# Transformer block on one core: 80 of 2048 units of the softmax exponentials computed on VectorE instead of ScalarE

## The chip, the cores and the metric

The kernel runs on one core of a Trainium2 chip. The metric is the device time of one execution in microseconds; the median of the runs counts. Engines are named as in the profile: PE (TensorE, with PEld for its weight loads), ACT (ScalarE), DVE (VectorE), POOL (GpSimd), SP (SyncE, whose queue issues the DMAs here).

## The reference

One block without learned norm weights, in bf16, for a sequence of 2048 tokens and width 640: attention with 32 heads of 20 elements, then a gated product with inner width 1728. Both have a layer norm ahead of them and a residual around them.

```python
h  = x + A(layernorm(x))        # A: qkv = x @ wqkv; p = softmax(q k^T * 20**-0.5); (p v) @ wo
h2 = h + B(layernorm(h))        # B: ((x @ w_gate) * (x @ w_up)) @ w_down
```

There are 32 x 2048 x 2048 exponentials. There is no mask, and the kernel subtracts no maximum: it checks at the end that the sums are in range, and has a slow general version for the case that they aren't (not run with these inputs).

## The kernel before

**Heads.** Four heads form a head group, eight groups in all (`NG`). In `qa`, `qb` and `kT` each head has a slot of 32 partitions, 20 with data and 12 of padding, so that a group fills 128 partitions. The values `vx` have 20 columns of data and one of ones per head, so that the product with them also gives the softmax's sum.

**Units, tiles, segments, passes.** The scores are made transposed, keys on partitions. A unit is one head, 128 keys and 512 queries: one score matmul (line 392), 512 exponentials per partition, and one matmul with the values (line 483, "AV"). Three units fill a tile of 1536 columns: PSUM tile `sc`, double buffered, is read by one ScalarE instruction that writes `E` in bf16:

```python
nc.scalar.activation(e[:, 0:n], sc[:, 0:n], ACT.Exp, scale=SM_SCALE)     # line 398
```

A segment is one head group against all its keys for one block of 512 queries: 16 key tiles x 4 heads = 64 units, collected in PSUM tile `acc` (one buffer). Pass "0" covers queries 0 to 511, "1" and "2" the next blocks; the last block is done as "3" for groups 0 and 1 and in halves "A" and "B" for the others. In pass 0 the groups 0 to 3 are done by key chunks, while the keys are still being made, with partial sums in `parts`. That leaves 20 whole segments of 64 units in the passes 0, 1 and 2: 4 + 8 + 8. The whole has 2048 units in 683 tiles.

**The order around it.** The program is emitted by one loop over tiles, and each engine executes in the order of emission. An iteration emits the three score matmuls and the exponential of tile i (`emit_S`), then the rest of a started job up to 640 ns of matmul time (`go_on`, `BUDGET`), then four AV matmuls of an older tile (`emit_AV`), then a piece of auxiliary VectorE work (`step_aux`) and due events. If no job was under way, it begins the next one (`begin`, up to `START` = 440 ns). So a projection of five matmuls takes two iterations.

**Jobs.** All other matmul work is a queue of jobs: transposes of the normalised input, the q, k and v projections (`job_proj`, `job_V`), then for each finished block of queries the tail: output projection with residual into `h` (`job_out`, line 697), layer norm on VectorE in pieces (`ln2_pieces`, lines 162 to 207), transposes, the gated product (`job_glu`, lines 757 and 764) and the last product (`job_y`, line 792). Each sum of a job goes through the one PSUM bank `mi` and is evacuated by VectorE (`evac`, line 223), which frees the bank for the next job. If a tile of scores needs a q or k that isn't made, `ensure` emits its job at once.

**Normalisation.** A finished segment is copied from `acc` to `asb` (line 491); its sums go through DRAM, their reciprocals come back as `bc`, five and then eight tiles later (`norm`, `later`), and VectorE's product (line 422) writes the bf16 result `On`, of which there are two sets, for even and odd blocks of queries. In three places where there is no time for that, it is done with small matmuls (`job_norm`).

The residual of the tail is loaded into `xr` (bf16), `h` is a tile of its own in fp32, and the output is written over `xr`.

Of the kernel before, what the change touches and what calls it, by code (L numbers as in the profile page):

```python
# [51 lines left out]
LAG = 10  # L52
EARLY = 48


@with_exitstack
def kernel(
# [23 lines left out]
    ep = pool("ep", 6)  # L81
    nrm = pool("nrm", 2)
    small = pool("small", 2)
    accp = pool("accp", 1, space=bass.MemoryType.PSUM)
# [10 lines left out]
    ext = const.tile([P, 4], F32, name="ext")  # L95
    bad = const.tile([1, 1], I32, name="bad")
    wo = [const.tile([P, D], BF16, name=f"wo{g}") for g in range(NG)]
    N_SUMS = 16 * (NB * NG)
# [6 lines left out]
    vx = [vp.tile([P, VW], BF16, name=f"vx{t}") for t in range(NT)]  # L105
    On = [[onp.tile([P, QB], BF16, name=f"on{s}_{g}") for g in range(NG)] for s in range(2)]

    lnT = ra.tile([P, KT, S], BF16, name="lnT")
    wv = [ra.tile([P, D], BF16, name=f"wv{c}") for c in range(KT)]
    wqk = [ep.tile([P, EW], BF16, name="E") for c in range(KT)]  # L110
    parts = [ra.tile([P, QB], F32, name=f"part{g}") for g in range(G1)]
    wpad = [ra.tile([P, 2, H, SLOT], BF16, name=f"wp{c}") for c in range(KT)]
# [30 lines left out]
    warm = small.tile([P, 1], BF16, name="warm")  # L143
    nc.scalar.activation(warm[:], ones[:], ACT.Sqrt)
    for c in range(KT):
        nc.vector.memset(wpad[c][:].rearrange("p m h e -> p (m h) e")[:, :, DH:SLOT], 0.0)
# [61 lines left out]

    lns = {}

    def apply1(t, m32, r, k, eng=None):
# [7 lines left out]
    def evac(eng, dst, src):  # L219
        if eng == "act":  # L220
            nc.scalar.copy(dst, src)
        else:
            nc.vector.tensor_copy(dst, src)  # L223

# [60 lines left out]
    FAST = {("2", NG - 1), ("A", NG - 1), ("B", NG - 2)}  # L285

    tiles, cur_t, pos = [], [], 0
    for s, (p, g, lo, hi, _) in enumerate(segs):
        w = PASS[p][2]
        n = BANK // w  # L290
        for kt, j, k in [(kt, j, k) for kt in range(lo, hi, n) for j in range(HPG) for k in range(n)]:
            cur_t.append((s, kt + k, j, pos))
            pos += w
            if pos == EW:
                tiles.append((cur_t, EW))
                cur_t, pos = [], 0
    if cur_t:
        tiles.append((cur_t, pos))

    av_q = deque()  # L300
# [7 lines left out]
    cur = {"key": None, "gen": None, "fresh": True}  # L308
    now = {"i": 0}
    col = {"n": 0}  # L310
# [71 lines left out]
    def emit_S(i):  # L382
        sc = scp.tile([P, EW], F32, name="sc")
        us, n = tiles[i]
        for s, kt, j, _ in us:
            p, g = segs[s][0:2]
            ensure(("k", g, kt // TPB))
            ensure(("q", PASS[p][0], g))
        for s, kt, j, o in us:
            p, g = segs[s][0:2]  # L390
            b, c0, w = PASS[p]
            nc.tensor.matmul(  # L392
                sc[:, o:o + w],
                lhsT=kT[g][SLOT * j:SLOT * (j + 1), kt * P:(kt + 1) * P],
                rhs=q_of(g, b, c0, w)[SLOT * j:SLOT * (j + 1), :],
                start=True, stop=True)
        e = ep.tile([P, EW], BF16, name="E")
        nc.scalar.activation(e[:, 0:n], sc[:, 0:n], ACT.Exp, scale=SM_SCALE)  # L398
        for s, kt, j, o in us:
            av_q.append((i, s, kt, j, e[:, o:o + PASS[segs[s][0]][2]]))  # L400

    def norm(s, asb):
        p, g = segs[s][0:2]
        b, c0, w = PASS[p]
        n = w // 32
        r16 = sums_all[:, col["n"]:col["n"] + n]
        col["n"] += n
        sums = dram.tile([HPG, w], F32, name="sums", tag=f"sums{w}")
        nc.sync.dma_start(sums[:], asb[DH:P:SLOT, 0:w])
        nc.sync.dma_start(r16, sums[:].rearrange("j (c f) -> (j c) f", f=n))  # L410

        def back():
            ri = nrm.tile([P, n], F32, name="ri", tag=f"ri{n}")
            nc.vector.reciprocal(ri[:], r16)
            scr = dram.tile([HPG, w], F32, name="scr", tag=f"scr{w}")
            nc.sync.dma_start(scr[:].rearrange("j (c f) -> (j c) f", f=n), ri[:])
            bc = nrm.tile([P, QB], F32, name="bc")
            for j in range(HPG):
                nc.sync.dma_start(bc[SLOT * j:SLOT * (j + 1), 0:w], scr[j:j + 1, :].to_broadcast([SLOT, w]))

            def mult():
                nc.vector.tensor_tensor(On[b % 2][g][:, c0:c0 + w], asb[:, 0:w], bc[:, 0:w], ALU.mult)  # L422
                done.add(("n", p, g))
            later(8, mult)
        later(5, back)
# [21 lines left out]
    def job_norm(s, asb):  # L447
# [5 lines left out]
        ps = rows_to_cols(bc, w, bank())  # L453
        nc.vector.tensor_tensor(On[b % 2][g][:, c0:c0 + w], asb[:, 0:w], ps[:, 0:w], ALU.mult)
        done.add(("n", p, g))
# [4 lines left out]
    def emit_AV(upto):  # L460
        if not av_q:
            return
        i, s = av_q[0][0:2]
        p, g, lo, hi, kind = segs[s]
# [14 lines left out]
        for _ in range(ready):  # L479
            _, _, kt, j, e = av_q.popleft()  # L480
            ensure(("v", kt, g // (NG // 2)))
            h = HPG * g + j
# [4 lines left out]
        acc["left"] -= ready  # L487
        if acc["left"] == 0:
            if kind in ("copy", "only"):
                asb = parts[g] if kind == "copy" else nrm.tile([P, QB], F32, name="asb")  # L490
# [36 lines left out]
    keep_busy(WARM)  # L527

    def ln_bank(k):
# [41 lines left out]
    load_x(2)  # L571
    evac("act", kT[0][:, 0:QB], pK[:, 0:QB])
    evac("dve", q_of(0, 0, 0, QB), pQ[:, 0:QB])
    done.update({("q", 0, 0), ("k", 0, 0)})
# [114 lines left out]
    def out_mm(on, st, t):  # L689
        for hf in range(2):  # L690
            ps = bank()
            cs = slice(hf * HALF, (hf + 1) * HALF)
            for g in range(NG):
                nc.tensor.matmul(ps[:, 0:HALF], lhsT=on[g][:, t * P:(t + 1) * P], rhs=wo[g][:, cs],  # L694
                                 start=(g == 0), stop=(g == NG - 1))
                if g == NG - 1:
                    nc.vector.tensor_tensor(st["h"][t][:, cs], ps[:, 0:HALF], st["xr"][t][:, cs], ALU.add)  # L697
                yield 136
# [16 lines left out]
    def job_out(on, st, ts, key):  # L715
# [10 lines left out]
        for k, pair in enumerate(pairs):  # L726
            for t in pair:
                yield from out_mm(on, st, t)
            if k:
                yield from T_pair(pairs[k - 1])  # L730
# [21 lines left out]
    def glu_sum(st, fp, f2, k, c0, n, hold):  # L752
# [3 lines left out]
        for c in range(KT):  # L756
            nc.tensor.matmul(ps[0:M, 0:n], lhsT=st["w", fp][k][:, c, f2 * P:f2 * P + M],  # L757
                             rhs=st["ln2T"][:, c, c0:c0 + n], start=(c == 0), stop=(c == KT - 1))
            if c == KT - 1:
                if k == 0:  # L760
                    u = hold["u"] = late["s"].tile([P, QB], BF16, name="u")
                    evac("dve" if end["pool"] is None else "act", u[0:M, 0:n], ps[0:M, 0:n])
                else:
                    nc.vector.tensor_tensor(st["hh"][2 * fp + f2][0:M, c0:c0 + n], ps[0:M, 0:n], hold["u"][0:M, 0:n], ALU.mult)  # L764
            yield 216 * n // QB
# [15 lines left out]
    def job_y(st, ts, store_halves=False):  # L781
        for t in ts:
            o = st["xr"][t]
            for hf in range(2):
                ps = bank()
                cs = slice(hf * HALF, (hf + 1) * HALF)
                for f in range(2 * FP):
                    K = min(P, FF - f * P)
                    nc.tensor.matmul(ps[:, 0:HALF], lhsT=st["hh"][f][0:K, t * P:(t + 1) * P],  # L789
                                     rhs=late["Wd"][f][0:K, cs], start=(f == 0), stop=(f == 2 * FP - 1))  # L790
                    if f == 2 * FP - 1:
                        nc.vector.tensor_tensor(o[:, cs], ps[:, 0:HALF], st["h"][t][:, cs], ALU.add)  # L792
                    yield 136
# [14 lines left out]
    def add_tail(b, ts):  # L808
# [13 lines left out]
        do(("load",) + key, ready)  # L822
        add(("out",) + key, lazy(lambda st: job_out(On[b % 2], st, ts, key)))
        add(("glu",) + key, lazy(lambda st: job_glu(st, ts)))
# [26 lines left out]
    def last_tail():  # L851
        st = tail_st[LAST_B]
        on = On[LAST_B % 2]
        asb = final["asb"]
# [57 lines left out]
    def flag_ok():  # L912
# [7 lines left out]
        ok = small.tile([P, 1], BF16, name="ok", tag="den")  # L920
        nc.vector.tensor_tensor(ok[:], lo[:], hi[:], ALU.mult)
        return ok

# [12 lines left out]
    while i < n_tiles or av_q:  # L936
        now["i"] = i
        if i < n_tiles:
# [39 lines left out]
    def general():  # L978
        st = new_st(None)
        st["res"] = {}  # L980
        with tc.For_i(0, S, P) as r0:
# [3 lines left out]
            for g in range(NG):  # L985
# [41 lines left out]
                nc.tensor.transpose(ps[:], oq[:].rearrange("p j e -> p (j e)"), ident[:])  # L1027
                nc.vector.tensor_copy(On[0][g][:, 0:P], ps[:])
            for fn in (job_out(On[0], st, [0], None), job_glu(st, [0]), job_y(st, [0])):
                for _ in fn:  # L1030
# [34 lines left out]
```

## Time and profile before

| | us |
|---|---|
| median of 3 runs (lowest, highest) | 998.93 (998.02, 999.89) |
| the profiled execution: its time | 1005.19 |
| the profiled execution: its span | 1003.4 |
| mean granted PE clock in it | 0.869 |

The profile is of one execution. Its span is what the page's shares refer to; 1.8 us of the run lie around it. A line such as `L398 ACT ACTIVATE E<-sc 128x1536 bf16<-128x1536 f32 x682` is a group of instructions: source line, engine, operation, output and input tile, shape, count; then the busy time, the mean duration of one in ns, and the idle time of the engine ahead of them with what ended it. Durations of neighbours can overlap, and a record can begin while the instruction ahead still runs. In rows of a timeline the first two numbers are start and length in us, and neighbouring records of one kind are merged. In the page's slices each digit is the busy share of a fortieth of the span in tenths.

### The profile page before, as it was taken

Reading aid. Unit: us, or ns where it says so; the run is one execution under the profiler, and the core shown is the slowest. Engines: PE = TensorE matmul, PEld = TensorE weight load, DVE = VectorE, ACT = ScalarE, POOL = GpSimd, SP = SyncE. Lnnn points to the kernel's source line nnn. Section 1 sums busy time; section 2 is a strip of 40 time slices with the busy share of each in tenths; the row PEclk is TensorE's granted clock in tenths of the full one; section 3 lists DMA queues with packets and bytes.
Section 4 is the critical chain, followed back from the end, with each engine's and each line's share of the span. In section 5 each row is a group of like instructions: output and inputs, shape, how many; then the busy total and the mean of one; then the engine's idle time right before and its main releaser. Section 6 shows DMA issues by size and latency. Waiting matters only on the chain.

```text
span 1003.4 us, 17152 instructions
## 1 busy us (share of the span) xinstructions
PE 889.1 (89%) x6985; PEld 333.2 (33%) x7041; DVE 313.7 (31%) x743; ACT 939.6 (94%) x719; POOL 20.2 (2%) x120
## 2 busy tenths in 40 slices
PE   7879999999698999977798999977798999989987
PEld 5223342233132223311132233421242333434455
DVE  7664343433044322100025332100034232233333
ACT  6779999999999999999999999999999999999951
POOL 5110000000000000000000000000000000000000
PEclk9889999999587999955577999965587999989989
DMA  6000010103421220100021220100501100112310
GB/s 178 27 1 1 1 37 12 45 12 143 129 63 49 79 58 19 32 12 12 8 59 38 65 75 22 33 13 6 143 20 40 37 14 8 38 47 61 84 34 16
DMA packets 67812, 44.39 MB, mean 44 GB/s; under 512 B 18504, under 2 KB 63404, under 8 KB 67728
## 3 DMA queue, kind: packets, MB, share of 16 engines
q1 hardware_dynamic: 67728, 43.23, 15.6%
q8 instruction: 57, 0.93, 0.4%
q14 instruction: 27, 0.22, 0.1%
HBM read 35.91 MB, written 7.30 MB: 43 GB/s over the span
## 4 chain that ended last, share of the span: by engine, by line
ACT 59%; PE 23%; issue 12%; DVE 5%; DMA 1%; ACTq 0%
ACT E L398 59%; PE sc L392 5%; PE acc L483 3%; PE mi L757 3%; PE mi L254 3%; PE mi L694 2%; PE f L757 2%; PE mi L264 1%; PE f L789 1%; DVE st L162 1%; PE mi L236 1%; DVE xs L215 1%; DVE kT L223 0%; DVE vx L223 0%; DVE xs L214 0%
## 5 line engine op out<-in xcount | busy, mean ns | idle before, releaser
L398 ACT ACTIVATE E<-sc 128x1536 bf16<-128x1536 f32 (+1 forms) x683 | 922.2, 1717 | 23.9 <-PE sc L392 21.1
L392 PE MATMUL sc<-qa,kT 32*128 32x512 bf16 x1536 | 234.4, 445 | 71.6 <-ACT E L398 63.3
L483 PE MATMUL acc<-E,vx 128*32 128x512 bf16 (+1 forms) x2432 | 234.3, 401 | 1.9 <-ACT E L398 1.1
L392 PEld LDWEIGHTS <-kT 32*128 32x128 bf16 x2432 | 98.4, 93 | 298.8 <-issue 285.8
L483 PEld LDWEIGHTS <-vx 128*32 128x32 bf16 x2432 | 56.9, 95 | 169.1 <-issue 164.8
L254 PE MATMUL mi<-lnT,wp 128*128 128x512 bf16 x284 | 87.0, 390 | 6.6 <-DVE lnT L223 1.3
L392 PE MATMUL sc<-qb,kT 32*128 32x256 bf16 (+1 forms) x896 | 72.7, 304 | 11.0 <-ACT E L398 9.6
L789 PE MATMUL mi<-wd,hh 128*128 128x320 bf16 x378 | 68.9, 304 | 0.1
L223 DVE CAST u<-mi 128x512 bf16<-128x512 f32 (+3 forms) x56 | 35.0, 624 | 92.7 <-PE mi L757 92.7
L764 DVE TENSOR_TENSOR hh<-mi,u 128x512 bf16<-128x512 f32 (+3 forms) x56 | 35.0, 624 | 86.8 <-PE mi L757 86.8
L491 DVE COPY asb<-acc 128x512 f32<-128x512 f32 (+1 forms) x34 | 20.2, 595 | 123.2 <-PE acc L483 123.2
L757 PE MATMUL mi<-ln2T,wu 128*128 128x512 bf16 (+2 forms) x186 | 53.6, 381 | 2.6 <-issue 0.7
L757 PE MATMUL mi<-ln2T,wg 128*128 128x512 bf16 (+2 forms) x191 | 52.6, 369 | 1.3 <-DMA wg<-in_B_w_gate_dram 0.4
L789 PEld LDWEIGHTS <-hh 128*128 128x128 bf16 x448 | 37.0, 98 | 37.1 <-issue 26.7
L694 PE MATMUL mi<-wo,on 128*128 128x320 bf16 x224 | 43.6, 321 | 0.0
L792 DVE TENSOR_TENSOR xr<-mi,h 128x320 bf16<-128x320 f32 x27 | 13.3, 492 | 84.6 <-PE mi L789 84.6
L223 DVE CAST kT<-mi 128x512 bf16<-128x512 f32 x31 | 21.4, 690 | 49.8 <-PE mi L254 49.7
L254 PEld LDWEIGHTS <-wp 128*128 128x128 bf16 x310 | 22.6, 97 | 41.0 <-issue 33.0
L757 PE MATMUL mi<-ln2T,qa 128*128 128x256 bf16 (+3 forms) x153 | 33.9, 326 | 1.5 <-DVE u L223 0.5
L264 PE MATMUL mi<-wv,lnT 128*128 128x320 bf16 x160 | 28.2, 308 | 4.7 <-DVE vx L223 4.2
L697 DVE TENSOR_TENSOR h<-mi,xr 128x320 f32<-128x320 f32 x28 | 13.8, 492 | 55.6 <-PE mi L694 55.1
L422 DVE TENSOR_TENSOR on<-asb,bc 128x512 bf16<-128x512 f32 (+1 forms) x30 | 18.1, 604 | 30.5 <-DMA bc<-scr 30.5
(128 smaller groups left out, 405.1 us busy)
## 6 DMA issues: line engine op xcount, KB each, us to landing
bc<-scr SPq DMA_DIRECT2D x100, 64.0 KB
wu<-in_B_w_up_dram SPq DMA_DIRECT2D x20, 320.0 KB
wg<-in_B_w_gate_dram SPq DMA_DIRECT2D x20, 320.0 KB
qsp<-qa SPq DMA_DIRECT2D x8, 384.0 KB
xr<-in_A_x_dram SPq DMA_DIRECT2D x16, 160.0 KB
out_dram<-xr SPq DMA_DIRECT2D x14, 160.0 KB
wd<-in_B_w_down_dram SPq DMA_DIRECT2D x13, 160.0 KB
xs<-in_A_x_dram SPq DMA_DIRECT2D x3, 640.0 KB
```

The lines of the kernel that those rows point to most:

```text
L223: nc.vector.tensor_copy(dst, src)
L254: nc.tensor.matmul(ps[:], lhsT=wslice(m, g, c), rhs=lnT[:, c, ch * QB:(ch + 1) * QB], start=(c == 0), stop=(c == KT - 1))
L264: nc.tensor.matmul(ps[:, 0:HALF], lhsT=lnT[:, c, t * P:(t + 1) * P], rhs=wv[c][:, half * HALF:(half + 1) * HALF], start=(c == 0), stop=(c ...
L392: nc.tensor.matmul(sc[:, o:o + w], lhsT=kT[g][SLOT * j:SLOT * (j + 1), kt * P:(kt + 1) * P], rhs=q_of(g, b, c0, w)[SLOT * j:SLOT * (j + 1) ...
L398: nc.scalar.activation(e[:, 0:n], sc[:, 0:n], ACT.Exp, scale=SM_SCALE)
L422: nc.vector.tensor_tensor(On[b % 2][g][:, c0:c0 + w], asb[:, 0:w], bc[:, 0:w], ALU.mult)
L483: nc.tensor.matmul(acc["t"][SLOT * j:SLOT * (j + 1), 0:w], lhsT=vx[kt][:, VS * h:VS * h + SLOT], rhs=e, start=(kt == lo), stop=(kt == hi - 1))
L491: nc.vector.tensor_copy(asb[:, 0:w], acc["t"][:, 0:w])
L694: nc.tensor.matmul(ps[:, 0:HALF], lhsT=on[g][:, t * P:(t + 1) * P], rhs=wo[g][:, cs], start=(g == 0), stop=(g == NG - 1))
L757: nc.tensor.matmul(ps[0:M, 0:n], lhsT=st["w", fp][k][:, c, f2 * P:f2 * P + M], rhs=st["ln2T"][:, c, c0:c0 + n], start=(c == 0), stop=(c == ...
L764: nc.vector.tensor_tensor(st["hh"][2 * fp + f2][0:M, c0:c0 + n], ps[0:M, 0:n], hold["u"][0:M, 0:n], ALU.mult)
L789: nc.tensor.matmul(ps[:, 0:HALF], lhsT=st["hh"][f][0:K, t * P:(t + 1) * P], rhs=late["Wd"][f][0:K, cs], start=(f == 0), stop=(f == 2 * FP ...
```

## The change

In the 20 whole segments of passes 0, 1 and 2, the four units of key tile 2 (`X_KT`), one per head, no longer go through ScalarE. The other 60 units of these segments are packed into tiles as before, so that there are 656 tiles.

**The new units.** For each, `emit_x` makes the score matmul into the bank `mi`, in an iteration that would else begin a job, from eight tiles ahead of the segment on and one every five tiles (`X_AHEAD`, `X_STEP`). VectorE then works on it in six passes over 128x512: one that reads the bank at once, and five more that `step_x` emits in later iterations, one or two in each (one, if the iteration already has another VectorE evacuation). Their AV matmuls are put at the end of their segment.

**The arithmetic.** The first pass multiplies the score by 2^23 / ln 2 x 20^-0.5 and converts it to an integer, whose upper bits are then the exponent of the result and whose lower 23 bits its fraction. Two passes separate them with bit operations (fraction as an fp32 in 1 to 2; exponent as an fp32 power of two), two evaluate the cubic's inner part, and the last adds the constant and multiplies by the power of two.

**What goes with it.** The integer has to be positive with the right exponent bias, so 394 is added to every score: `one_row` and `shift_row` hold 1 and 394 in the first padding row of each slot, and the evacuations of q and k add them (a `tensor_scalar` with a per-partition operand instead of a copy, line 278 of the changed kernel). The exponentials that stay on ScalarE take that and the cubic's leading factor out by a bias, a column `ebias` in SBUF. A check is added at the end that an overlarge value converts to the largest integer.

**Memory.** `h` is now written in bf16 over `xr`; there is one set of `On` instead of two, so that the product of one block waits until the previous block's output projection has been emitted (`("om", b)`); `parts` lies in the unused part of `qa`.

```diff
+SHIFT = 394.0
+X_AHEAD, X_STEP, X_OUT = 8, 5, 6
+X_SCALE = SM_SCALE * LOG2E * 2.0 ** 23
+C3 = 0.07802454279127117
+X_P, X_Q, X_R = -0.10261439735317812, 6.123365857342997, 5.794771205884579
+EXP_BIAS = (SHIFT * SM_SCALE * LOG2E - 127.0) / LOG2E - math.log(C3) - SHIFT * SM_SCALE
...
-    On = [[onp.tile([P, QB], BF16, name=f"on{s}_{g}") for g in range(NG)] for s in range(2)]
+    On = [onp.tile([P, QB], BF16, name=f"on{g}") for g in range(NG)]
...
+    nc.gpsimd.memset(ebias[:], EXP_BIAS)
...
-                evac("dve", kT[g][:, ch * QB:(ch + 1) * QB] if m else q_of(g, ch, 0, QB), ps[:])
+                now["ev"] += 1
+                nc.vector.tensor_scalar(kT[g][:, ch * QB:(ch + 1) * QB] if m else q_of(g, ch, 0, QB), ps[:],
+                                        (one_row if m else shift_row)[:, 0:1], None, ALU.add)
...
+            if s in X_SEGS and X_KT <= kt < X_KT + n:
+                continue
...
-        nc.scalar.activation(e[:, 0:n], sc[:, 0:n], ACT.Exp, scale=SM_SCALE)
+        nc.scalar.activation(e[:, 0:n], sc[:, 0:n], ACT.Exp, bias=ebias[:], scale=SM_SCALE)
...
+    def emit_x():
...
+        ps = bank()
...
+            nc.tensor.matmul(
+                ps[:, k * w:(k + 1) * w],
+                lhsT=kT[g][SLOT * j:SLOT * (j + 1), (X_KT + k) * P:(X_KT + k + 1) * P],
+                rhs=q_of(g, b, c0, w)[SLOT * j:SLOT * (j + 1), :],
+                start=True, stop=True)
...
+        nc.vector.tensor_scalar(v[:], ps[:], X_SCALE, 0.0, ALU.mult, ALU.max)
...
+        def last():
+            nc.vector.scalar_tensor_tensor(e[:], t[:], X_R, v[:].bitcast(F32), ALU.add, ALU.mult)
...
+        x_pieces.extend([
+            lambda: nc.vector.tensor_scalar(m[:].bitcast(I32), v[:], 0x007FFFFF, 0x3F800000, ALU.bitwise_and, ALU.bitwise_or),
+            lambda: nc.vector.tensor_scalar(v[:], v[:], 0x7F800000, None, ALU.bitwise_and),
+            lambda: nc.vector.scalar_tensor_tensor(t[:], m[:], X_P, m[:], ALU.add, ALU.mult),
+            lambda: nc.vector.scalar_tensor_tensor(t[:], t[:], X_Q, m[:], ALU.add, ALU.mult),
+            last])
...
             def mult():
-                nc.vector.tensor_tensor(On[b % 2][g][:, c0:c0 + w], asb[:, 0:w], bc[:, 0:w], ALU.mult)
+                if b and ("om", b - 1) not in done:
+                    later(1, mult)
+                    return
+                nc.vector.tensor_tensor(On[g][:, c0:c0 + w], asb[:, 0:w], bc[:, 0:w], ALU.mult)
...
-    evac("act", kT[0][:, 0:QB], pK[:, 0:QB])
+    nc.scalar.activation(kT[0][:, 0:QB], pK[:, 0:QB], ACT.Identity, bias=one_row[:, 0:1])
...
-        st["h"] = [hp.tile([P, D], F32, name=f"h{t}") for t in range(TPB)]
...
+        st["h"] = st["xr"]
...
+        step_x(1 if now["ev"] else 2)
         if not used:
-            begin(START)
+            if x_todo and cur["fresh"] and x_ready():
+                emit_x()
+            else:
+                begin(START)
```

More of the change, by code (lines that the diff above doesn't have):

```diff
@@ L1 @@
+import math
 from collections import deque
@@ L53 @@
 EARLY = 48
+SHIFT = 394.0
+X_AHEAD, X_STEP, X_OUT = 8, 5, 6
+LOG2E = 1.4426950408889634
+X_SCALE = SM_SCALE * LOG2E * 2.0 ** 23
+C3 = 0.07802454279127117
+X_P, X_Q, X_R = -0.10261439735317812, 6.123365857342997, 5.794771205884579
+EXP_BIAS = (SHIFT * SM_SCALE * LOG2E - 127.0) / LOG2E - math.log(C3) - SHIFT * SM_SCALE
 @with_exitstack
@@ L82 @@
     nrm = pool("nrm", 2)
+    xp = pool("xp")
     small = pool("small", 2)
@@ L96 @@
     bad = const.tile([1, 1], I32, name="bad")
+    one_row = const.tile([P, 1], F32, name="one_row")
+    shift_row = const.tile([P, 1], F32, name="shift_row")
+    ebias = const.tile([P, 1], F32, name="ebias")
+    huge = const.tile([P, 1], F32, name="huge")
     wo = [const.tile([P, D], BF16, name=f"wo{g}") for g in range(NG)]
@@ L110 @@
     wqk = [ep.tile([P, EW], BF16, name="E") for c in range(KT)]
-    parts = [ra.tile([P, QB], F32, name=f"part{g}") for g in range(G1)]
+    parts = [qa[g][:, QB:QA].bitcast(F32) for g in range(G1)]
     wpad = [ra.tile([P, 2, H, SLOT], BF16, name=f"wp{c}") for c in range(KT)]
@@ L144 @@
     nc.scalar.activation(warm[:], ones[:], ACT.Sqrt)
+    nc.gpsimd.memset(ebias[:], EXP_BIAS)
+    nc.gpsimd.memset(huge[:], 3.0e38)
     for c in range(KT):
@@ L209 @@
     lns = {}
+    now = {"i": 0, "ev": 0}
     def apply1(t, m32, r, k, eng=None):
@@ L257, in job_proj @@
             if c == KT - 1:
-                evac("dve", kT[g][:, ch * QB:(ch + 1) * QB] if m else q_of(g, ch, 0, QB), ps[:])
+                if not m and 0 < ch < NB - 1 and g < G1:
+                    assert ("n", "0", g) in done
+                now["ev"] += 1
+                nc.vector.tensor_scalar(kT[g][:, ch * QB:(ch + 1) * QB] if m else q_of(g, ch, 0, QB), ps[:],
+                                        (one_row if m else shift_row)[:, 0:1], None, ALU.add)
             yield 216
@@ L285 @@
     FAST = {("2", NG - 1), ("A", NG - 1), ("B", NG - 2)}
+    X_KT = 2
+    X_SEGS = [s for s, (p, g, _, _, kind) in enumerate(segs)
+              if kind == "only" and p in "012"]
     tiles, cur_t, pos = [], [], 0
@@ L298 @@
         tiles.append((cur_t, pos))
+    first_tile = {}
+    for i, (us, _) in enumerate(tiles):
+        for s, *_ in us:
+            first_tile.setdefault(s, i)
+    x_todo = deque((first_tile[s] - X_AHEAD + X_STEP * j, s, j) for s in X_SEGS for j in range(HPG))
+    x_pieces = deque()
+    x_made = {}
+    x_live = {"units": 0, "passes": 0}
     av_q = deque()
@@ L308 @@
     cur = {"key": None, "gen": None, "fresh": True}
-    now = {"i": 0}
     col = {"n": 0}
@@ L397, in emit_S, with x_ready @@
         e = ep.tile([P, EW], BF16, name="E")
-        nc.scalar.activation(e[:, 0:n], sc[:, 0:n], ACT.Exp, scale=SM_SCALE)
+        nc.scalar.activation(e[:, 0:n], sc[:, 0:n], ACT.Exp, bias=ebias[:], scale=SM_SCALE)
         for s, kt, j, o in us:
             av_q.append((i, s, kt, j, e[:, o:o + PASS[segs[s][0]][2]]))
+    def x_ready():
+        due, s, _ = x_todo[0]
+        p, g = segs[s][0:2]
+        return (due <= now["i"] and x_live["units"] < X_OUT and x_live["passes"] < 2
+                and ("q", PASS[p][0], g) in done and ("k", g, 0) in done)
@@ new lines, in emit_x @@
+    def emit_x():
+        _, s, j = x_todo.popleft()
+        p, g = segs[s][0:2]
+        b, c0, w = PASS[p]
+        n = BANK // w
+        ensure(("k", g, X_KT // TPB))
+        ensure(("q", b, g))
+        ps = bank()
+        for k in range(n):
+            nc.tensor.matmul(
[3 more added lines that the diff above has]
+                start=True, stop=True)
+        v = xp.tile([P, BANK], I32, name="xv", bufs=2)
+        m = xp.tile([P, BANK], F32, name="xm")
+        t = xp.tile([P, BANK], F32, name="xt")
+        e = xp.tile([P, BANK], BF16, name="xe", bufs=X_OUT)
+        now["ev"] += 1
+        nc.vector.tensor_scalar(v[:], ps[:], X_SCALE, 0.0, ALU.mult, ALU.max)
+        x_live["units"] += 1
+        x_live["passes"] += 1
+        def last():
+            nc.vector.scalar_tensor_tensor(e[:], t[:], X_R, v[:].bitcast(F32), ALU.add, ALU.mult)
+            x_live["passes"] -= 1
+            x_made.setdefault(s, []).append((j, e))
+            if len(x_made[s]) == HPG:
+                put = [(now["i"], s, X_KT + k, j, e[:, k * w:(k + 1) * w]) for k in range(n) for j, e in x_made[s]]
+                at = next((k for k, u in enumerate(av_q) if u[1] > s), len(av_q))
+                for u in reversed(put):
+                    av_q.insert(at, u)
+        x_pieces.extend([
[4 more added lines that the diff above has]
+            last])
@@ L402, in norm, with step_x, need_x @@
+    def step_x(n):
+        while n > 0 and x_pieces:
+            x_pieces.popleft()()
+            n -= 1
+    def need_x(s):
+        while len(x_made.get(s, ())) < HPG:
+            if x_pieces:
+                step_x(1)
+                continue
+            while not cur["fresh"]:
+                step()
+            emit_x()
     def norm(s, asb):
@@ L453, in job_norm @@
         ps = rows_to_cols(bc, w, bank())
-        nc.vector.tensor_tensor(On[b % 2][g][:, c0:c0 + w], asb[:, 0:w], ps[:, 0:w], ALU.mult)
+        assert b == 0 or ("om", b - 1) in done
+        nc.vector.tensor_tensor(On[g][:, c0:c0 + w], asb[:, 0:w], ps[:, 0:w], ALU.mult)
         done.add(("n", p, g))
@@ L462, in emit_AV @@
             return
+        if acc["seg"] is not None and av_q[0][1] != acc["seg"]:
+            need_x(acc["seg"])
         i, s = av_q[0][0:2]
@@ L480, in emit_AV @@
             _, _, kt, j, e = av_q.popleft()
+            if s in X_SEGS and kt == X_KT:
+                x_live["units"] -= 1
             ensure(("v", kt, g // (NG // 2)))
@@ L488, in emit_AV @@
         if acc["left"] == 0:
+            now["ev"] += 1
             if kind in ("copy", "only"):
@@ L527 @@
     keep_busy(WARM)
+    nc.vector.tensor_reduce(one_row[:], ident[:, DH::SLOT], axis=AX.X, op=ALU.add)
+    nc.vector.tensor_scalar(shift_row[:], one_row[:], SHIFT, None, ALU.mult)
     def ln_bank(k):
@@ L571 @@
     load_x(2)
-    evac("act", kT[0][:, 0:QB], pK[:, 0:QB])
-    evac("dve", q_of(0, 0, 0, QB), pQ[:, 0:QB])
+    nc.scalar.activation(kT[0][:, 0:QB], pK[:, 0:QB], ACT.Identity, bias=one_row[:, 0:1])
+    nc.vector.tensor_scalar(q_of(0, 0, 0, QB), pQ[:, 0:QB], shift_row[:, 0:1], None, ALU.add)
     done.update({("q", 0, 0), ("k", 0, 0)})
@@ L696, in out_mm @@
                 if g == NG - 1:
+                    now["ev"] += 1
                     nc.vector.tensor_tensor(st["h"][t][:, cs], ps[:, 0:HALF], st["xr"][t][:, cs], ALU.add)
@@ L728, in job_out @@
                 yield from out_mm(on, st, t)
+            if key is not None and k == len(pairs) - 1:
+                done.add(("om", key[0]))
             if k:
@@ L763, in glu_sum @@
                 else:
+                    now["ev"] += 1
                     nc.vector.tensor_tensor(st["hh"][2 * fp + f2][0:M, c0:c0 + n], ps[0:M, 0:n], hold["u"][0:M, 0:n], ALU.mult)
@@ L791, in job_y @@
                     if f == 2 * FP - 1:
+                        now["ev"] += 1
                         nc.vector.tensor_tensor(o[:, cs], ps[:, 0:HALF], st["h"][t][:, cs], ALU.add)
@@ L822, in add_tail @@
         do(("load",) + key, ready)
-        add(("out",) + key, lazy(lambda st: job_out(On[b % 2], st, ts, key)))
+        add(("out",) + key, lazy(lambda st: job_out(On, st, ts, key)))
         add(("glu",) + key, lazy(lambda st: job_glu(st, ts)))
@@ L852, in last_tail @@
         st = tail_st[LAST_B]
-        on = On[LAST_B % 2]
+        on = On
         asb = final["asb"]
@@ L921, in flag_ok @@
         nc.vector.tensor_tensor(ok[:], lo[:], hi[:], ALU.mult)
+        top = small.tile([P, 1], I32, name="top", tag="nt")
+        nc.vector.tensor_scalar(top[:], huge[:], 1.0, 0.0, ALU.mult, ALU.max)
+        nc.vector.tensor_scalar(lo[:], top[:], 2.0e9, None, ALU.is_ge)
+        nc.vector.tensor_tensor(ok[:], ok[:], lo[:], ALU.mult)
         return ok
@@ L936 @@
     while i < n_tiles or av_q:
-        now["i"] = i
+        now["i"], now["ev"] = i, 0
         if i < n_tiles:
@@ L958 @@
             a_seen = True
+        step_x(1 if now["ev"] else 2)
         if not used:
-            begin(START)
+            if x_todo and cur["fresh"] and x_ready():
+                emit_x()
+            else:
+                begin(START)
         i += 1
@@ L1027, in general @@
                 nc.tensor.transpose(ps[:], oq[:].rearrange("p j e -> p (j e)"), ident[:])
-                nc.vector.tensor_copy(On[0][g][:, 0:P], ps[:])
-            for fn in (job_out(On[0], st, [0], None), job_glu(st, [0]), job_y(st, [0])):
+                nc.vector.tensor_copy(On[g][:, 0:P], ps[:])
+            for fn in (job_out(On, st, [0], None), job_glu(st, [0]), job_y(st, [0])):
                 for _ in fn:
```

## The prediction

> **What bounds the kernel now.** I read the page's busy line and its slices first, then the chain, then ScalarE's and VectorE's own rows.
>
> ```profile
> PE 889.1 (89%) x6985; PEld 333.2 (33%) x7041; DVE 313.7 (31%) x743; ACT 939.6 (94%) x719; POOL 20.2 (2%) x120
> ...
> DVE  7664343433044322100025332100034232233333
> ACT  6779999999999999999999999999999999999951
> ...
> PEclk9889999999587999955577999965587999989989
> ...
> ACT 59%; PE 23%; issue 12%; DVE 5%; DMA 1%; ACTq 0%
> ```
>
> ScalarE is busy 94% of the span, at 9 in 35 of 40 slices, and leads the chain. VectorE has two thirds of its time free. PE's 89% counts stretched time: where VectorE is at 0 or 1, no projection or tail work is left, and PE runs at half clock without making ScalarE wait. The windows show that (columns: stretch, total, then PE, PEld, DVE, ACT, POOL busy with counts, clock, DMA share, GB/s):
>
> ```profile
> 136.00:255.00 119.00, 110.04 (x754) 36.88 (x764) 41.82 (x74) 119.00 (x90) 0.00 (x0) 1.00 0.19 60
> ...
> 400.00:510.00 110.00, 88.06 (x574) 26.25 (x572) 9.31 (x18) 110.00 (x83) 0.00 (x0) 0.62 0.10 28
> ```
>
> So an exponential taken off ScalarE is worth its full time in nearly all of the middle, and one made longer costs its full time too. Hence ScalarE's timeline, in two stretches:
>
> ```profile
> 353.10 28.64 ACT L398 ACTIVATE E<-sc 128x1536 bf16<-128x1536 f32 x21
> ...
> 969.33 1.13 ACT L891 ACTIVATE ln<-f,mr,rstd 128x320 bf16<-128x320 f32 x2 [0.48 <-DVE mr L886]
> ...
> 971.59 1.42 ACT L897 COPY h<-f 128x320 f32<-128x320 f32 x4
> ```
>
> The 21 exponentials start from 353.10 to 379.72 (the line's own view names first and last start): 20 intervals in 26.62, **1.331 us** a tile of 1536. A record lasts longer, 1.7 to 2.0 us, since it begins while the previous one runs; the distance between starts is what counts.
>
> **ScalarE: what is taken away.** 80 units of 512 leave; 683 tiles become 656, or 26.7 full tiles fewer: 26.7 x 1.331 = **-35.5 us**.
>
> **ScalarE: what is added.** Line 398 had an immediate bias; every one of the 656 exponentials now has `bias=ebias[:]`, a column in SBUF read per partition. No exponential of before has one, so I take the price from the two rows above, both 320 elements from PSUM, back to back. The four copies have no such operand: 1.42 less the last one's 0.45 leaves three intervals, 0.323 each. The two of L891 have two, bias and scale: 1.13 less 0.619 gives 0.511. The difference is 0.188, or **0.094 us per operand**, and it shows between starts, so the overlap of neighbours doesn't hide it. The durations alone (0.615 against 0.450) give 0.082. That the exponential of before pays for no such operand fits too: with the slope of ScalarE's casts, (586 - 377) / 256 = 0.816 ns an element, 0.323 leaves 0.062 for a copy and 1.331 leaves 0.078 for it. So 656 x 0.094 = **+61.7 us**; lower end 656 x 0.082 = 53.8, upper end the same 61.7, and nothing at all is a rival below. I take 0.094, since starts, not durations, set the pace.
>
> The Trainium skill, in "ScalarE: Activation LUTs", section "What ACT_TABLE_LOAD costs", says that each such pointer operand adds about 93 ns to an ACTIVATE, and that one with immediates takes 186 ns + 0.833 ns an element with neighbours overlapping by 93 ns. By that an exponential would go from 1.373 to 1.466 and the two steps above would sum to 656 x 1.466 - 682.7 x 1.373 = +24 us, estimated from that page; by the rows it is +26.2. The page's 1.373 disagrees with the trace's 1.331, which decides.
>
> **Where ScalarE wasn't the bound.** The price falls only on intervals that ScalarE sets. From first start 15.44 to last 959.8 the starts lie 36.6 us over 1.331 each: 23.9 of it is the idle time of the group's row (21.1 waiting for line 392), most at the start and where the block tail begins on a cold PE. Taken start by start, only 27.8 us lie above 1.425. The 8.8 between is slack that the longer exponential uses up: **-8.8 us** (0 to -8.8).
>
> **VectorE.** A unit is one pass from PSUM and five in SBUF on 128x512. Prices by form:
>
> ```profile
> L491 DVE COPY asb<-acc 128x512 f32<-128x512 f32 x22 | 15.2, 689 | 110.3 <-PE acc L483 110.3
> ...
> L422 DVE TENSOR_TENSOR on<-asb,bc 128x512 bf16<-128x512 f32 x21 | 14.4, 685 | 30.5 <-DMA bc<-scr 30.5
> ...
> L207 DVE TENSOR_SCALAR ln<-h,m,rstd 128x640 bf16<-128x640 f32 x14 | 8.4, 604 | 0.2
> ```
>
> The PSUM pass is like L491, 0.69. The three scalar_tensor_tensor passes read two SBUF streams like L422, 0.69 each. The two bit passes read one stream: L207 does 640 elements in 0.604 with two operands per partition, and the SBUF copy of L438 does 512 in 0.43, so 0.43, with 0.69 the upper end. A unit is 0.69 + 2 x 0.43 + 3 x 0.69 = 3.62 us, all 80 are 290 us (331 at most), and DVE goes to about 600 us of the span. It is not the bound on average. By stage: a segment of a changed head group is 20 tiles, 28.5 us at 1.425. The instruction order of the changed kernel puts a unit into every fifth tile with two projections between: 4 x 3.62 = 14.5, eight evacuations of 0.74, and 1.6 for asb, product and reciprocal make 22, or 77%. Where the block tail's layer norm falls (25 to 28.5 us of 28.5 by the rows' prices) the queue is full: an evacuation behind one or two passes holds the only `mi` bank, and PE's next group, then the scores, wait. I price it at **+3 us**, between 0 (all fits in the 1.425) and +10 (0.3 us at each of some 30 evacuations of two such stages). The addition in 63 evacuations costs VectorE (0.600 of L890 - 0.492 of L697) / 2 = 0.054 each, 3.4 us, hidden outside the start.
>
> **PE and the queue of jobs.** Scores and AV of the 80 units stay on PE; each score matmul takes an otherwise free job slot. That delays jobs by 80 slots, with 27 tiles fewer. By the instruction order, before had some 135 tiles without a job matmul in its three long gaps (the 0s and 1s of the DVE row), so the jobs still end in time. One gap, 255 to 280, closes, and with it a restart of PE at half clock: three intervals of 2.27, 1.72 and 2.15, so **-1.9 us** over 1.425. Cover gone would mean scores waiting for q or k, 1 us each; the order shows none.
>
> **The rest.** At the start two small VectorE instructions precede the first bn_stats (0.16 each), ScalarE's first kT evacuation gets a pointer (0.09), and the first evacuations are longer: **+1 us** (0 to 2). h in bf16: a row of 0.492 either way (L697 f32, L792 bf16), nothing. One set of On: the product of a pass's first group waits some tiles for the previous out stage; only the next tail, over 100 tiles later, reads it. Three tiny checks at the end lie under the last GLU. Nothing for these.
>
> **Sum**: -35.5 + 61.7 - 8.8 + 3 - 1.9 + 1 = **+19.5 us**. The profiled execution has a span of 1003.4 in a run of 1005.19, 0.6% over the median 998.93; I add the sum to the median: **1018 us**. Ends: 0.082 instead of 0.094 takes 8 off, VectorE 3 and the start 1 more, 1006; no slack used and VectorE's +10 give 1034.
>
> **Rivals.** *The operand is free (faster, 10%).* An exponential's record starts 0.4 to 0.7 us before its predecessor ends; if the column were fetched then, every tile would stay at 1.331. For it: those long records, and a price that rests on one pair of instructions. Against: that pair overlapped too (0.611 with 0.511 between starts) and still paid. It gives -35.5 + 3 - 1.9 + 1 = -33, 966 us. The sign turns where 656 times the price equals the 33 plus the slack used up, at about 0.06 us.
>
> *VectorE's queue becomes the bound (slower still, 10%).* If the bit passes take 0.69 and each of the 80 units puts one 0.69 pass ahead of an evacuation, beyond PE's free 0.25 us a tile (1.425 less scores 0.33, AV 0.25 and two or three job matmuls 0.6), that is 80 x 0.44 = 35 at worst; half of it, 18, gives 1036. For it: one `mi` bank. Against: a job finishes every second tile and leaves over 1 us for the queue to drain.
>
> *Both halves cancel (2%)*: at a price near those 0.06 us the time stays at 999.
>
> **Chances.** The forecast has 78%: slower. Slower in all 88%, the same 2%, faster 10%; 0.2%, some 2 us, is about what a measurement of this kernel tells from no change. The range takes the forecast's ends, 2 us more below because one profiled execution stands for all, and the near half of the VectorE case: 1004 to 1036. Outside are the free operand, no change and the far half, 17%.
>
> **What would show it.** In the changed profile: exponentials 1.42 apart in a stretch like 353 to 380, 656 of them, ScalarE still at 9 in the middle; the five pass lines at 0.43 and 0.69; DVE near 600 us; few waits of PE for VectorE. If the exponentials stand at 1.331, the forecast is wrong in sign; if ScalarE's idle time grows far over 24 us, VectorE's queue is why.

## The result and the profile after

The changed kernel takes **1049.32 us** (median of 4 runs, 1048.55 to 1054.77) against 999.41 (998.02 to 1001.76): a ratio of **1.0512**, 95% interval 1.0473 to 1.0551. It is slower, as forecast, but by 49.9 us where the forecast had 19.5. The profiled executions differ by as much: spans of 1052.9 and 1003.4.

From the page of the changed kernel, the busy line, slices and chain that answer to those of before:

```profile
PE 894.6 (85%) x7041; PEld 337.0 (32%) x7041; DVE 586.7 (56%) x1228; ACT 961.8 (91%) x692; POOL 20.2 (2%) x122
...
DVE  6654377777735977766557777766234232133233
ACT  6889999999956999999999899999999999999961
...
PEclk9989999999977799999768699999697999989999
...
ACT 40%; PE 24%; issue 22%; DVE 10%; SPq 2%; DMA 2%; DVEq 0%; ACTq 0%
...
L433 ACT ACTIVATE E<-sc,ebias 128x1536 bf16<-128x1536 f32 x656 | 944.4, 1713 | 51.1 <-PE sc L427 47.2
```

VectorE went from 313.7 to 586.7 us, and ScalarE, with 27 instructions fewer, from 939.6 up to 961.8. Two things are new: a hole in ScalarE's row, the 5 and 6 at slices 12 and 13, and idle time of 51.1 us ahead of the exponentials where before had 23.9.

ScalarE's timeline of the changed kernel, in a stretch with no such hole:

```profile
606.70 30.20 ACT L433 ACTIVATE E<-sc,ebias 128x1536 bf16<-128x1536 f32 x21
```

The last of the 21 starts at 635.16, so 20 intervals take 28.46: **1.423 us** a tile against 1.331, 0.092 more. The passes on VectorE, by form (mean ns behind the busy time):

```profile
L480 DVE SCALAR_TENSOR_TENSOR xt<-xt,xm 128x512 f32<-128x512 f32 x80 | 55.2, 691 | 2.6
L468 DVE SCALAR_TENSOR_TENSOR xe<-xt,xv 128x512 bf16<-128x512 f32 x80 | 55.1, 689 | 2.0
L463 DVE TENSOR_SCALAR xv<-mi 128x512 int32<-128x512 f32 x80 | 55.0, 687 | 40.1 <-PE mi L453 35.7 <-PE sc L427 4.3
L479 DVE SCALAR_TENSOR_TENSOR xt<-xm 128x512 f32<-128x512 f32 x80 | 54.5, 681 | 0.0
L478 DVE TENSOR_SCALAR xv<-xv 128x512 int32<-128x512 int32 x80 | 34.2, 427 | 2.8
L477 DVE TENSOR_SCALAR xm<-xv 128x512 int32<-128x512 int32 x80 | 34.0, 425 | 2.5
```

These are 288 us, each pass at its forecast price. So the sum's two big terms hold, and the missing 30 us are waits. The hole in ScalarE's row, in the timeline of the changed kernel (start, length, then in brackets the engine's idle time before and what ended it):

```profile
322.00 0.49 DVE L805 TENSOR_TENSOR xr<-mi,xr 128x320 bf16<-128x320 f32 x1 [22.22 <-DMA xr<-in_A_x_dram]
...
322.54 1.22 PE L801 MATMUL mi<-wo,on 128*128 128x320 bf16 x4 [20.15 <-DVE xr L805]
...
324.41 1.54 ACT L433 ACTIVATE E<-sc,ebias 128x1536 bf16<-128x1536 f32 x1 [19.94 <-PE sc L427]
```

VectorE waits 22.2 us for the residual `xr` of the first block tail; behind it the `mi` bank stays full, PE stands, no scores are made, and ScalarE runs dry. SP's own timeline around it shows what stands ahead of the load:

```profile
300.36 0.43 SPq L757 DMA_DIRECT2D qsp<-qa  x1
...
310.63 7.16 SPq L776 DMA_DIRECT2D wd<-in_B_w_down_dram  x14
317.85 1.99 SPq L788 DMA_DIRECT2D xr<-in_A_x_dram  x4
```

Sixteen stores of q and fourteen loads of `wd` are issued between 300.36 and 317.79, and the four loads of `xr` come only then. In the kernel before, the same transfers lay apart:

```profile
251.40 0.94 SPq L651 DMA_DIRECT2D qsp<-qb  x1
...
267.80 6.65 SPq L669 DMA_DIRECT2D wd<-in_B_w_down_dram  x14
274.49 2.01 SPq L682 DMA_DIRECT2D xr<-in_A_x_dram  x4
...
277.60 1.25 PE L694 MATMUL mi<-wo,on 128*128 128x320 bf16 x4
...
280.67 0.49 DVE L697 TENSOR_TENSOR h<-mi,xr 128x320 f32<-128x320 f32 x1 [10.46 <-PE mi L694]
```

The first row is the last of the sixteen stores, which were issued from 241.3 on, beside the last projections. The loads of `wd` and `xr` fell into the gap of 255 to 280, in which PE had no job to do, and the first use of `xr` at 280.67 waited for PE alone.

### The profile page after: what moved, and what is told of

The parts are those of the page before. It is cut to its first block, busy times and chain, and to the rows that moved or that the text cites. A ratio compares the mean times of both kernels' runs of the same rounds, so it can differ in the third digit from the quotient of the medians.

```text
span 1052.9 us, 17606 instructions
## 1 busy us (share of the span) xinstructions
PE 894.6 (85%) x7041; PEld 337.0 (32%) x7041; DVE 586.7 (56%) x1228; ACT 961.8 (91%) x692; POOL 20.2 (2%) x122
## 4 chain that ended last, share of the span: by engine, by line
ACT 40%; PE 24%; issue 22%; DVE 10%; SPq 2%; DMA 2%; DVEq 0%; ACTq 0%
ACT E L433 40%; PE sc L427 5%; PE acc L586 4%; PE mi L867 3%; PE mi L271 2%; PE mi L801 2%; PE mi L900 2%; PE f L867 1%; PE mi L285 1%; DVE st L177 1%; DVE xv L463 1%; SPq L745 1%; PE f L900 1%; PE mi L253 1%; DVE xt L480 1%
## 5 line engine op out<-in xcount | busy, mean ns | idle before, releaser
L433 ACT ACTIVATE E<-sc,ebias 128x1536 bf16<-128x1536 f32 x656 | 944.4, 1713 | 51.1 <-PE sc L427 47.2
L427 PE MATMUL sc<-qa,kT 32*128 32x512 bf16 x1456 | 209.5, 412 | 72.1 <-ACT E L433 67.4
L586 PE MATMUL acc<-E,vx 128*32 128x512 bf16 (+1 forms) x2352 | 217.0, 379 | 2.2 <-ACT E L433 1.5
L427 PE MATMUL sc<-qb,kT 32*128 32x256 bf16 (+1 forms) x896 | 73.1, 304 | 22.2 <-ACT E L433 17.7
L463 DVE TENSOR_SCALAR xv<-mi 128x512 int32<-128x512 f32 x80 | 55.0, 687 | 40.1 <-PE mi L453 35.7
L480 DVE SCALAR_TENSOR_TENSOR xt<-xt,xm 128x512 f32<-128x512 f32 x80 | 55.2, 691 | 2.6
L468 DVE SCALAR_TENSOR_TENSOR xe<-xt,xv 128x512 bf16<-128x512 f32 x80 | 55.1, 689 | 2.0
L479 DVE SCALAR_TENSOR_TENSOR xt<-xm 128x512 f32<-128x512 f32 x80 | 54.5, 681 | 0.0
L904 DVE TENSOR_TENSOR xr<-mi,xr 128x320 bf16<-128x320 f32 x27 | 13.3, 492 | 66.2 <-PE mi L900 66.2
L805 DVE TENSOR_TENSOR xr<-mi,xr 128x320 bf16<-128x320 f32 x28 | 13.7, 491 | 55.0 <-PE mi L801 29.8
L278 DVE TENSOR_SCALAR kT<-mi,one_row 128x512 bf16<-128x512 f32 x31 | 23.2, 748 | 35.6 <-PE mi L271 35.4
L453 PE MATMUL mi<-qa,kT 32*128 32x512 bf16 x80 | 32.3, 404 | 7.8 <-DVE xr L805 3.4
```

The source lines that it names most:

```text
L427: nc.tensor.matmul(sc[:, o:o + w], lhsT=kT[g][SLOT * j:SLOT * (j + 1), kt * P:(kt + 1) * P], rhs=q_of(g, b, c0, w)[SLOT * j:SLOT * (j + 1) ...
L433: nc.scalar.activation(e[:, 0:n], sc[:, 0:n], ACT.Exp, bias=ebias[:], scale=SM_SCALE)
L463: nc.vector.tensor_scalar(v[:], ps[:], X_SCALE, 0.0, ALU.mult, ALU.max)
L468: nc.vector.scalar_tensor_tensor(e[:], t[:], X_R, v[:].bitcast(F32), ALU.add, ALU.mult)
L479: lambda: nc.vector.scalar_tensor_tensor(t[:], m[:], X_P, m[:], ALU.add, ALU.mult),
L480: lambda: nc.vector.scalar_tensor_tensor(t[:], t[:], X_Q, m[:], ALU.add, ALU.mult),
```

## The experiments

Each experiment has its own runs of the kernel before on the same chip: 1001.38 us for the first four, 1000.27 for the next four, 1000.67 for the last three. What an experiment is worth is told as the distance of its median from the median of that before; the changed kernel's is +49.9. The ratios beside are the record's own and differ from the quotient of the medians by up to 0.3%. Their intervals are 2 to 4.5 us to either side, so a difference of two distances is known to some 4 or 5 us.

**The column alone.** To the kernel before, only the per-partition bias is added.

```diff
+    nc.gpsimd.memset(ebias[:], 0.0)
...
-        nc.scalar.activation(e[:, 0:n], sc[:, 0:n], ACT.Exp, scale=SM_SCALE)
+        nc.scalar.activation(e[:, 0:n], sc[:, 0:n], ACT.Exp, bias=ebias[:], scale=SM_SCALE)
```

> The kernel before, with one thing added: the bias of the 683 exponentials is a column of zeros in SBUF instead of the immediate 0. Theory of the operand: the starts of the exponentials move from 1.331 to 1.423 us in the stretches that ScalarE sets, 683 x 0.092 = 62.8 us, less the 8.8 us of slack that I took as used up: about +54, 1053 us. Rival, that the operand costs only with the other work of the change beside it: no change, 999 us. If no slack is used up: +63, 1062 us.

Measured: 1057.48 us, ratio 1.0557 (1.0526 to 1.0588), +56.1. Its ScalarE timeline:

```profile
353.34 28.86 ACT L400 ACTIVATE E<-sc,ebias 128x1536 bf16<-128x1536 f32 x20
```

The last of these 20 starts at 380.4: 19 intervals of 1.42. The column costs its 0.092 with nothing else changed. Of the 62.8 us that 683 of them make, 6.7 do not show in the time; I put them down to the slack. That the operand is free is refuted.

**The bias as a number.** In the changed kernel, an immediate in place of the column.

```diff
-        nc.scalar.activation(e[:, 0:n], sc[:, 0:n], ACT.Exp, bias=ebias[:], scale=SM_SCALE)
+        nc.scalar.activation(e[:, 0:n], sc[:, 0:n], ACT.Exp, bias=EXP_BIAS, scale=SM_SCALE)
```

> The changed kernel with the bias as an immediate number; all else stays. Theory of the operand: starts back at 1.331, 656 x 0.092 = 60 us less on ScalarE, of which the shorter tiles give some 10 to 15 back, since VectorE and PE then have 0.09 us less in each: 1049 - 48 = about 1001 us (995 to 1008), so no better than before, because the wait for the residual (22 us) and VectorE's queue stay. Rival, that the 50 us come from VectorE's queue and the operand is hidden: within 10 us of 1049.

Measured: 1003.44 us, ratio 1.0019 (1.0000 to 1.0038), +2.1: 47.8 us less than with the column, and about level with before. The long wait for `xr` is still there, 22.0 us in this kernel's trace.

**The residual first.** The loads of `wd` and the stores of q go behind the loads of `xr` in the queue of jobs.

```diff
-    for g in range(NG):
-        do(("spill", g), lambda g=g: spill(g))
...
         do(("load",) + key, ready)
+        if b == 0:
+            do(("wd",), load_wd)
+            for g in range(NG):
+                do(("spill", g), lambda g=g: spill(g))
```

> The changed kernel with another order of jobs: the four loads of the residual xr stand ahead of the 14 loads of wd and the 16 stores of q, which they follow in the changed kernel. Theory of the queue: the 22.2 us in which VectorE, then PE, then ScalarE wait for xr fall to the 3 to 5 us that four issues and one landing take, so 16 to 19 us less: about 1031 us. Rival, that the DMA is slow itself (the engines busy with 2 MB of stores and loads): the wait stays over 12 us and the time over 1039.

Measured: 1030.09 us, ratio 1.0276 (1.0247 to 1.0305), +28.7: 21.2 us less than the changed kernel. SP's timeline of this kernel, and from its list of waits VectorE's for `xr` (total, times, longest):

```profile
298.51 1.80 SPq L788 DMA_DIRECT2D xr<-in_A_x_dram  x4
```

```profile
DVE xr L805 <- DMA xr<-in_A_x_dram: 5.7, 2, 3.0
```

The two waits come to 5.7 us where the changed kernel's came to 25.0, and the longest is 3.0 in place of 22.2. The same bytes move in another order, so the transfers ahead of `xr` are shown as the cause. Whether SP's issuing or the transfers themselves set their pace, this run can't tell, since `xr` now goes ahead of both. The windows speak for the transfers (columns as in the prediction's windows; the last but one is the DMA share), first two of the changed kernel, then one of this one:

```profile
302.00:312.00 10.00, 0.39 (x7) 0.19 (x5) 0.00 (x0) 2.48 (x2) 0.00 (x0) 0.61 1.00 379
312.00:322.00 10.00, 0.00 (x0) 0.00 (x0) 0.00 (x1) 0.00 (x0) 0.00 (x0) 0.50 0.95 290
```

```profile
300.00:322.00 22.00, 18.07 (x137) 6.88 (x134) 16.65 (x45) 21.26 (x15) 0.00 (x0) 0.93 1.00 346
```

The DMA engines were busy 95 to 100% of the time from 302 to 322. By the page's list of issues the stores of q and loads of `wd` are 6256 KB, three times the 2 MB that I had named. With `xr` first the engines are just as busy, but PE and ScalarE work beside them.

**Both edits.**

> Both edits: bias as an immediate and xr loaded first. If the two causes are separate, the gains add: 1049 - 48 - 18 = about 983 us (975 to 992), below the 999 of the kernel before. If the longer exponential had covered part of the same waits, under 60 us are gained and it stays above 990.

Measured: 983.03 us, ratio 0.9804 (0.9775 to 0.9834), -18.4. The gains add: 49.9 - 47.8 - 21.2 is -19.1. This version is faster than the kernel before, by 1.5 to 2.3% if its second measurement (below) is taken in.

**Without five of the six passes, with the column** (and `xr` first). The pass from PSUM writes the bf16 result itself, so the 80 units' values are no exponentials; matmuls, evacuations and the other 656 exponentials stay.

```diff
-        nc.vector.tensor_scalar(v[:], ps[:], X_SCALE, 0.0, ALU.mult, ALU.max)
+        nc.vector.tensor_scalar(e[:], ps[:], 1.0, 0.0, ALU.mult, ALU.max)
...
-        x_pieces.extend([
...
+        last()
```

> The changed kernel with xr loaded first, and five of the six VectorE passes of each unit left out: the pass from PSUM writes the unit's bf16 result itself, so the 80 units' values are not exponentials; 235 us of VectorE work are gone, all matmuls, evacuations and the 656 exponentials with their column stay. Theory of VectorE's queue: the time that the loads-first kernel (1030) has over the forecast (1018) is evacuations behind those passes, and it falls to 1015 to 1019. Rival, that it is cold PE or the extra job slots of the units: it stays above 1026.

Measured: 1020.22 us, ratio 1.0193 (1.0167 to 1.0219), +20.0: 8.7 us less than with the passes. ScalarE's waits for scores, first of the kernel with the passes, then of this one:

```profile
ACT E L433 <- PE sc L427: 25.1, 37, 2.9
```

```profile
ACT E L433 <- PE sc L427: 15.6, 19, 2.9
```

Half of the 37 waits go (18), and 9.5 us with them. The time is 1 us above what I expected, far below the rival's 1026.

**Without these passes, with the bias as a number** (and `xr` first).

> The same five passes left out of the kernel with both edits (immediate bias, xr first), 983 us. Theory of VectorE's queue: with tiles of 1.331 the queue has less room than with 1.423, so the passes cost more here than there: 14 to 18 us, to 965 to 969, which is about the 1001 of before less 26.7 x 1.331 = 35.5. Rival: no more than 5 us.

Measured: 969.40 us, ratio 0.9676 (0.9650 to 0.9702), -30.9: 12.5 us less than with the passes, a little under the 14 to 18 expected. That the passes cost more here than the 8.7 us with the column, because shorter tiles leave VectorE's queue less room, is not shown: the 3.8 us between are within what the intervals allow.

**All units on ScalarE**, with both edits and the rest of the change.

```diff
-              if kind == "only" and p in "012"]
+              if kind == "only" and p in ""]
```

> The kernel with both edits, but no units for VectorE: all 2048 units in 683 tiles on ScalarE. The shift by 394, the additions in the evacuations, h in bf16, the single set of On and the job order stay. If these cost nothing, as I had it: 1001 to 1004 us, the before of the same chip and some 1 us for the start. If the addition in the evacuations or the single On set holds something up: over 1006.

Measured: 1002.60 us, ratio 1.0008 (0.9990 to 1.0027), no difference that can be told. So the additions in 63 evacuations, `h` in bf16, one set of `On`, `parts` in `qa` and the order of loads cost nothing measurable. From here to 969.40 the 27 tiles fewer bring 33.2 us, of 35.5 at 1.331 each.

**Passes that yield.** With both edits, a piece of layer norm counts as VectorE work of its iteration.

```diff
-        step_aux()
+        busy_aux = step_aux()
...
-        step_x(1 if now["ev"] else 2)
+        step_x(2 - bool(now["ev"]) - bool(busy_aux))
```

> The kernel with both edits and one more: step_x also counts a piece of layer norm as VectorE work of its iteration, so it emits no pass in an iteration that has both an evacuation and such a piece. Theory of VectorE's queue: the stalls in the output projection stages (some 10 us of the 983) shrink by a third, to 978 to 981. Rival, that moving passes only moves the stall: within 2 us of 983.

Measured: 981.42 us, ratio 0.9804 (0.9759 to 0.9850), against 983.03. The intervals overlap, so both kernels ran again side by side.

> The same kernel as e8_yield, with more rounds beside the one without that edit: theory of VectorE's queue 2 to 4 us under it; rival, no difference that the rounds can tell.

> The same kernel as e4_both, as the other side of the comparison: 981 to 985 us.

Measured: 981.56 us, ratio 0.9812 (0.9792 to 0.9832), and without the edit 983.72, ratio 0.9832 (0.9812 to 0.9852). Some 2 us less both times, and the intervals overlap both times: not settled.

**At most one pass per iteration.**

```diff
-X_AHEAD, X_STEP, X_OUT = 8, 5, 6
+X_AHEAD, X_STEP, X_OUT = 10, 5, 6
...
-        step_x(1 if now["ev"] else 2)
+        step_x(0 if now["ev"] and busy_aux else 1)
```

> The kernel with both edits and a smoother feed of the passes: at most one per iteration, none in an iteration with both an evacuation and a piece of layer norm; units start ten instead of eight tiles ahead of their segment. Theory of VectorE's queue: stalls come from pairs of passes ahead of an evacuation, so of the 14 us between 983 and the 969 without passes a third to a half goes: 976 to 979. Rival, that only the sum of VectorE's work counts: 981 to 985.

Measured: 1012.99 us, ratio 1.0151 (1.0115 to 1.0187): 29 us over the kernel beside it, outside both expectations. From its list of waits, then one place of its timeline:

```profile
PE mi L867 <- DVE xv L463: 22.1, 22, 1.7
PE mi L271 <- DVE xv L463: 20.6, 18, 1.9
```

```profile
585.48 0.37 PE L453 MATMUL mi<-qa,kT 32*128 32x512 bf16 x1
...
585.94 0.68 DVE L480 SCALAR_TENSOR_TENSOR xt<-xt,xm 128x512 f32<-128x512 f32 x1
...
586.65 0.69 DVE L468 SCALAR_TENSOR_TENSOR xe<-xt,xv 128x512 bf16<-128x512 f32 x1
587.45 0.69 DVE L463 TENSOR_SCALAR xv<-mi 128x512 int32<-128x512 f32 x1
...
588.20 0.81 PE L867 MATMUL mi<-ln2T,wg 128*128 128x512 bf16 x3 [1.71 <-DVE xv L463]
```

At this place a unit's last two passes stand in front of the next unit's first one, which is what empties the bank, and PE's next job waits for that. With both edits alone the same two waits were far shorter:

```profile
PE mi L867 <- DVE xv L463: 3.3, 10, 0.6
PE mi L271 <- DVE xv L463: 2.8, 9, 0.6
```

So the stall needs no pairs of passes, as I had it; what counts in these rows is what stands ahead of the instruction that frees the bank. The run also starts its units two tiles earlier, and which of its edits brings how much of the 29 us is not separated.

## Why the prediction was right in sign and wrong in size

- **27 tiles fewer, -35.5**: right within what can be told; without the five passes and the column the units bring 33.2.
- **The column, +61.7**: right. 1.423 between starts, where 0.094 had given 1.425; 656 x 0.092 = 60.4. Two short instructions at the end of the trace had priced 656 long ones to 2%. The Trainium skill's rule ("ScalarE: Activation LUTs", section "What ACT_TABLE_LOAD costs") of about 93 ns for each pointer operand agrees with this 92; the 1.466 for a whole exponential, an estimate from the same section's figures, does not agree with 1.423.
- **Slack, -8.8**: near; 6.7 with the column alone.
- **VectorE's passes, +3**: a mis-sized term. Each pass was priced right (425 to 691 ns), but leaving five of them out brings 8.7 us, near the end that I had given as the upper. I had looked for them in the tail stages alone; they come among the projections too, as here in the changed kernel, where an evacuation of q behind three passes holds up PE:

```profile
229.78 0.69 DVE L479 SCALAR_TENSOR_TENSOR xt<-xm 128x512 f32<-128x512 f32 x1
...
230.50 0.69 DVE L480 SCALAR_TENSOR_TENSOR xt<-xt,xm 128x512 f32<-128x512 f32 x1
...
231.23 0.69 DVE L468 SCALAR_TENSOR_TENSOR xe<-xt,xv 128x512 bf16<-128x512 f32 x1
231.84 0.74 DVE L278 TENSOR_SCALAR qa<-mi,shift_row 128x512 bf16<-128x512 f32 x1
232.63 0.58 PE L453 MATMUL mi<-qa,kT 32*128 32x512 bf16 x1 [1.56 <-DVE qa L278]
```

- **PE and the queue of jobs, -1.9**: the step that failed. I had counted the jobs' matmuls and slots, found that the gap of 255 to 280 closes, and booked the end of a cold restart. I didn't look at the transfers that the same jobs issue on SP, 16 stores just ahead of that gap, 14 loads of `wd` and then `xr` in it. With the gap gone, they came all at once with the reader of `xr` right behind them. "Cover gone would mean scores waiting for q or k, 1 us each" named the wrong cover: the gap covered transfers, and putting `xr` first is worth 21.2 us. The slow restart that I had booked as gone came back behind the hole: four matmuls of the output projection take 1.22 us at 322.54, as the 1.25 at 277.60 in the kernel before, and 0.70 with `xr` first (at 301.40 of its trace).
- **The rest, +1**: right within what can be told, by the version with all units on ScalarE (ratio 0.9990 to 1.0027).

Of the 30.4 us between the sum and the result, the transfers ahead of `xr` make 21.2, the restart behind the hole with them, and VectorE's queue makes 5.7 beyond my 3. Left are 3.5, less than the runs can tell apart; 2.1 less of slack and 2.3 less for the tiles may be in them. The rival of a free operand fell with the column alone. The rival of VectorE's queue priced 18 more; it was there with a third of that, and didn't set the size. Its sign misled: ScalarE's idle time did grow far over 24 us, to 51.1, as I had written it would for VectorE's queue, but 19.94 of that is the one wait behind `xr`.

## What to carry to other kernels

Before an operand on the bounding engine becomes a per-partition column, ask whether it is a constant: here it is, and as a number it gave back 47.8 us. A gap without jobs isn't free to fill: list the DMAs issued in it or just ahead of it, in the order of their queue and with their bytes, and who waits for which of them. Where several kinds of work share one PSUM bank, price what stands in the evacuating engine's queue ahead of the instruction that frees the bank, not that engine's sum.

## What the runs showed of the hardware

The column's 0.092 us was paid in full although an exponential's record begins 0.1 to 0.3 us before its predecessor's ends (durations of 1.57 to 1.74 with 1.423 between starts): the overlap of the records hid nothing of it. On VectorE a column costs about 0.06: 748 ns for the k evacuation against 690 for the copy before and 687 for L463, a `tensor_scalar` with two numbers, all 128x512 from PSUM. The bit operations on int32 in SBUF take 425 to 427 ns for 512 elements, as little as the one-stream fp32 copy of L438. SP issued the 30 stores and loads in 17.4 us, 0.58 each, while the DMA engines were busy 0.95 to 1.00 of the time at 379 GB/s (302 to 312, mostly stores) and 290 (312 to 322, loads); so the 0.58 need not be the price of issuing alone.
